# A block of x loaded by itself, a stored block without its identity matmul, and the first chunk's scores packed into 15 batches for 16

## The chip, the cores and the metric

One core of a Trainium2 chip runs the kernel. The metric is the device time of one execution in microseconds (us). The kernel before took 268.93 us (median of 3 runs, 268.72 to 268.98). A program on one core has no second die to compare with. All medians below are of runs that were classed fast.

## The reference, cut to what matters

```python
def reference(A_x, A_wqkv, A_wo, B_x, B_w_gate, B_w_up, B_w_down):
    xn = _layernorm(A_x)                         # x: 1 x 2048 x 512, bf16
    # attention: 32 heads of 16, each query sees itself and the 255 keys before it
    q, k, v = split(xn @ wqkv)
    p = softmax(where(0 <= i - j < 256, q k^T / 4, -1e9))
    # gated block without a nonlinearity, F = 1792
    return A_x + (p v) @ wo + ((xn @ w_gate) * (xn @ w_up)) @ w_down
```

## The kernel before

The sequence is worked on in four chunks of 512 rows. In each chunk there are four groups `c` of eight heads. The scores of one group are computed in *batches*: up to 512 columns of queries against 64-key pieces, written to one PSUM tile `S` of four banks. ScalarE takes the exp of the whole tile into a strip `P`. GpSimd then cuts the far edge of the window (two instructions for each far block) and VectorE the diagonal.

```python
FIRST = (((5, 5, 7), (0, 0, 4)), ((3, 3, 5), (1, 1, 5)),
         ((3, 6, 7), (7, 7, 7), (2, 2, 6)), ((4, 4, 7), (6, 6, 7)))   # (key piece, first and last query block)

def scores(self, T, c, pieces):
    S = self.s_tiles.tile([128, 4, 512], F32, tag="S", name="S")     # one buffer
    ...                                                              # 16 small-tile matmuls for each piece
    P = self.ppool.tile([128, 4, 512], BF16, tag="P", name="P")      # seven buffers
    nc.scalar.activation(out=P[:, :, 0:col], in_=S[:, :, 0:col], func=ACT.Exp, scale=0.25)
    for at in self.places(pieces, 4):
        for half in (slice(0, 64), slice(64, 128)):
            self.triangle(P[half, :, at:at + 64], False)             # GpSimd: the far masks
```

All other matmuls (projections, gate, up, down, output) are *fillers*: a list that a small scheduler puts between the score batches when the program is built. It does so by estimated cost, so that the fillers are spread evenly over the batches:

```python
total = sum(w[0] for w in work) - RESERVE + SCORES * len(steps) + VALUES * (len(due) - 1)
for g, s in enumerate(steps):
    self.scores(*s)
    upto = total * (g + 1) / len(steps)
    ...
    fill(upto, g)               # fillers until the estimate says `upto`
    self.mask_diag(*s)
```

One filler of cost 0 opens the next chunk. It takes the chunk's tiles and has GpSimd fill the ones columns and the padding of `V`. The value projections come just behind it, and ScalarE copies their results into the other columns of `V`:

```python
def new_chunk(self, T):
    ...
    nc.gpsimd.memset(self.heads(self.V[T])[:, :, :, 16:18], 1.0)     # "the fills"
    nc.gpsimd.memset(self.V[T][:, VW - 16:], 0.0)
    nc.gpsimd.memset(self.VS[T][:, SW - 16:], 0.0)

def proj_v(self, t, ks=range(4)):
    ps = self.bank(ks, "vp")                                         # one of four PSUM banks ("M")
    ...                                                              # four matmuls
    nc.scalar.activation(out=heads(V[T])[...][:, :, :, 0:16], in_=ps, func=ACT.Copy)

def project(T):                                                      # in the list of fillers
    add(0, lambda: self.new_chunk(T))
    for b in range(4):
        ... proj_v ...
    ... proj_qk ...

gu(T, ...)                                                           # the gate and up matmuls of chunk T
if T + 1 < NCH:
    project(T + 1)
```

The softmax here doesn't subtract the row's maximum and nothing guards it: scores larger than these inputs give would overflow.

Of the kernel before, what the change touches and what calls it, by code (L numbers as in the profile page):

```python
# [7 lines left out]
BF16 = mybir.dt.bfloat16  # L8
# [7 lines left out]
BIG = 2.0 ** 126  # L16
VW = 4 * 32 * 18 + 16
SW = 4 * 16 * 18 + 16
FIRST = (((5, 5, 7), (0, 0, 4)), ((3, 3, 5), (1, 1, 5)),
         ((3, 6, 7), (7, 7, 7), (2, 2, 6)), ((4, 4, 7), (6, 6, 7)))  # L20
LATER = (((-2, 0, 2), (0, 0, 4)), ((5, 5, 7), (1, 1, 5)), ((-3, 0, 1), (7, 7, 7), (3, 3, 7)),
         ((-4, 0, 0), (6, 6, 7), (2, 2, 6)), ((-1, 0, 3), (4, 4, 7)))
ACT_FREE = 11


class Kernel:
# [26 lines left out]
    def setup(self):  # L53
        nc, const, NT, NF = self.nc, self.const, self.NT, self.NF
        self.x = const.tile([128, NT, 512], BF16, name="x")
        self.Wqkv = const.tile([128, 4, 1536], BF16, name="Wqkv")
        self.Wo = const.tile([128, 4, 512], BF16, name="Wo")
        self.Wg = const.tile([128, 4, self.F], BF16, name="Wg")
        self.Wu = const.tile([128, 4, self.F], BF16, name="Wu")
        self.Wd = const.tile([128, NF, 512], BF16, name="Wd")  # L60
        xv = self.x_d.rearrange("(t p) d -> p t d", p=128)
        wq = self.w_d["qkv"].rearrange("(k p) n -> p k n", p=128)
        wg = self.w_d["g"].rearrange("(k p) n -> p k n", p=128)
        wu = self.w_d["u"].rearrange("(k p) n -> p k n", p=128)
        for lo, hi in ((0, 1), (1, 4)):
            nc.sync.dma_start(out=self.x[:, lo:hi, :], in_=xv[:, lo:hi, :])
        for lo in (1024, 512, 0):
            nc.sync.dma_start(out=self.Wqkv[:, :, lo:lo + 512], in_=wq[:, :, lo:lo + 512])
        h = self.F // 2
        for lo in (0, h):  # L70
            nc.sync.dma_start(out=self.Wg[:, :, lo:lo + h], in_=wg[:, :, lo:lo + h])
            nc.sync.dma_start(out=self.Wu[:, :, lo:lo + h], in_=wu[:, :, lo:lo + h])
            if lo == 0:
                nc.sync.dma_start(out=self.x[:, 4:8, :], in_=xv[:, 4:8, :])
        nc.sync.dma_start(out=self.Wd[:], in_=self.w_d["d"].rearrange("(f p) n -> p f n", p=128))
        nc.sync.dma_start(out=self.Wo[:], in_=self.w_d["o"].rearrange("(c p) n -> p c n", p=128))
        nc.sync.dma_start(out=self.x[:, 8:NT, :], in_=xv[:, 8:NT, :])

        warm = const.tile([128, 1], F32, name="warm")
        nc.vector.memset(warm[:], 0.0)  # L80
        nc.scalar.activation(out=warm[:], in_=warm[:], func=ACT.Exp)
        ident = const.tile([128, 128], BF16, name="ident")
        nc.gpsimd.memset(ident[:], 0.0)
        nc.gpsimd.affine_select(out=ident[:], in_=ident[:], compare_op=ALU.not_equal, fill=1.0,
                                base=0, pattern=[[-1, 128]], channel_multiplier=1)
        self.ident = ident
        wps = self.ps_m.tile([128, 128], F32, tag="M", name="wps")
        for _ in range(38):
            nc.tensor.matmul(wps[:], lhsT=ident[:], rhs=ident[:], start=True, stop=True)
        pi = const.tile([128, 1], I32, name="pi")  # L90
        nc.gpsimd.iota(pi[:], pattern=[[0, 1]], base=0, channel_multiplier=1)
        podd = const.tile([128, 1], I32, name="podd")
        nc.vector.tensor_scalar(out=podd[:], in0=pi[:], scalar1=4, scalar2=1,
                                op0=ALU.arith_shift_right, op1=ALU.bitwise_and)
        self.odd = const.tile([128, 1], F32, name="odd")
        nc.vector.tensor_copy(out=self.odd[:], in_=podd[:])
        self.mhalf = const.tile([128, 4], F32, name="mhalf")
        nc.gpsimd.memset(self.mhalf[:], -0.5)
        self.diag = const.tile([128, 64], BF16, name="diag")
        self.far = const.tile([128, 64], BF16, name="far")  # L100
        nc.gpsimd.memset(self.diag[:], BIG)
        nc.gpsimd.memset(self.far[:], BIG)
        for half in (slice(0, 64), slice(64, 128)):
            self.triangle(self.diag[half], True)
            self.triangle(self.far[half], False)
        self.xnT, self.Q, self.hT, self.O, self.OT = {}, {}, {}, {}, {}
        self.K, self.Ko, self.V, self.VS = {}, {}, {}, {}
        self.strips, self.at = {}, {}

    def new_chunk(self, T):  # L110

# [135 lines left out]
        self.proj_qk(0, 1, 1)  # L247


    def scores(self, T, c, pieces):  # L250

        nc = self.nc
        S = self.s_tiles.tile([128, 4, 512], F32, tag="S", name="S")
        col = 0
        for m, q0, q1 in pieces:
            U, j = divmod(8 * T + m, 8)
            keys, q, n = slice(64 * j, 64 * j + 64), 64 * q0, 64 * (q1 - q0 + 1)
            for par in range(2):
                for e in range(4):
                    rows = slice(32 * e, 32 * e + 16 + 16 * par)  # L260
                    nc.tensor.matmul(S[64 * par:64 * par + 64, e, col:col + n],  # L261
                                     lhsT=(self.Ko if par else self.K)[U][rows, c, keys],
                                     rhs=self.Q[T][rows, c, q:q + n],
                                     start=True, stop=True, tile_position=(32 * e, 64 * par),
                                     skip_group_check=True)
            col += n
        P = self.ppool.tile([128, 4, 512], BF16, tag="P", name="P")
        nc.scalar.activation(out=P[:, :, 0:col], in_=S[:, :, 0:col], func=ACT.Exp, scale=0.25)  # L268
        self.strips[(T, c, pieces)] = P
        for at in self.places(pieces, 4):  # L270
            for half in (slice(0, 64), slice(64, 128)):
                self.triangle(P[half, :, at:at + 64], False)

    def places(self, pieces, far):

        out, at = [], 0
        for m, q0, q1 in pieces:
            out += [at + 64 * (q - q0) for q in range(q0, q1 + 1) if q == m + far]
            at += 64 * (q1 - q0 + 1)
        return out  # L280

    def mask_diag(self, T, c, pieces):

        P = self.strips[(T, c, pieces)]
        places = [at // 64 for at in self.places(pieces, 0)]
        step = places[1] - places[0] if len(places) == 2 else 1
        v = P.rearrange("p e (b x) -> p e b x", x=64)[:, :, places[0]:places[-1] + 1:step, :]
        n = len(places)
        self.nc.vector.tensor_tensor(out=v, in0=v, op=ALU.min,  # L289
                                     in1=self.diag.unsqueeze(1).unsqueeze(1).to_broadcast([128, 4, n, 64]))  # L290

    def values(self, T, c, accs=None):
# [2 lines left out]
        nc = self.nc  # L295
        if accs is None:
            accs = [self.ps_m.tile([128, 512], F32, tag="M", name="acc") for _ in range(2)]
        todo = []
        for pieces in LATER if T else FIRST:
            P, col = self.strips.pop((T, c, pieces)), 0  # L300
            for m, q0, q1 in pieces:
                todo.append((P, col, m, 64 * q0, 64 * (q1 - q0 + 1)))
                col += 64 * (q1 - q0 + 1)
        for i, (P, col, m, q, n) in enumerate(todo):
            U, j = divmod(8 * T + m, 8)
            b, h = divmod(j, 2)
# [99 lines left out]
    def fillers(self):  # L406


        out = []
        NCH, NF = self.NCH, self.NF  # L410

        def add(cost, f, before=None, after=None):
            out.append((cost, f, before, after))
# [65 lines left out]
        T = NCH - 1  # L479
        for b in range(4):  # L480
            down(T, b)
            if b < 3:
                wo(T, b, (0, 1, 2))
            if b in (1, 3):
                add(1, lambda b=b: self.add_x(T, b, 0 if b == 1 else 1))
        return [(*o, None, None)[:4] for o in out]

    def run(self):
# [5 lines left out]
        self.first_chunk()  # L494
        steps, self.first, self.last = [], {}, {}
        for T in range(NCH):
            for c in range(4):
                self.first[T, c] = len(steps)
                for pieces in LATER if T else FIRST:
                    self.last[T, c] = len(steps)  # L500
                    steps.append((T, c, pieces))
        due = {g: key for key, g in self.last.items()}
        SCORES, VALUES = 1.85, 5.5
        self.beside = {}
# [2 lines left out]
        spent, n, scored = 0, 0, 0  # L507
# [44 lines left out]
        T = NCH - 1  # L552
# [10 lines left out]
        fill(spent + 15, -1)  # L563
        for b in range(3):
            self.wo(T, b, (3,))
            self.store(T, b, on_act=(b == 1))
        fill(10 ** 9, -1)
        assert n == len(work)
        self.wo(T, 3, (0, 1, 2, 3))
# [39 lines left out]
```

## Time and profile before

| what | value | read from |
|---|---|---|
| device time, median | 268.93 us | timed runs |
| span of the profiled run (its device time 269.22) | 267.5 us | page |
| TensorE busy | 258.4 us, 97% | page, part 1 |
| 512-column matmuls, start to start | 0.2155 us | TensorE timeline |
| a score batch of 512 columns between fillers | 0.10 + 0.35 us | TensorE timeline |
| idle time of ScalarE before value copies, until GpSimd's fills | 1.4 us in all | waits |

Three lines of the page of the kernel before: the span, the first part (busy us, share of the span, instructions of each engine; PEld is the weight load) and the chain of waits by engine.

```profile
span 267.5 us, 8861 instructions
...
PE 258.4 (97%) x3860; PEld 119.1 (45%) x3882; DVE 181.7 (68%) x352; ACT 170.6 (64%) x132; POOL 113.8 (43%) x281
...
PE 88%; DVE 7%; issue 1%; DMA 1%; ACT 1%; SPq 0%; POOL 0%; DVEq 0%; POOLq 0%
```

TensorE is busy nearly all the time and is most of the chain, so the time is what TensorE needs before it is saturated, plus its work, plus the tail, plus any gaps.

The head, from the timeline of the kernel before. Columns: start, duration, engine, line, operation, output and inputs, count, and in brackets the idle time before it and what ended it. An entry that stands for several instructions runs from the first start to the last end, with others in between.

```profile
2.86 0.69 DVE L148 BATCH_NORM_STATS2 st<-x 128x6 f32<-128x512 bf16 x1 [1.02 <-DMA x<-in_A_x_dram]
...
4.80 0.70 DVE L148 BATCH_NORM_STATS2 st<-x 128x6 f32<-128x512 bf16 x1 [0.84 <-DMA x<-in_A_x_dram]
...
5.63 0.38 DVE L168 TENSOR_SCALAR xn<-x,mv,rs 128x512 bf16<-128x512 bf16 x1
...
7.25 0.40 PE L186 MATMUL xTp<-ident,xn 128*128 128x128 bf16 x4 [0.79 <-DVE xn L168]
...
7.49 0.81 PE L200 MATMUL vp<-Wqkv,xnT 128*128 128x512 bf16 x3
```

The statistics of block 1 (the second `st`) start at 4.80 us, after 0.84 us of waiting for the transfer of blocks 1 to 3. Block 0 is normalized only behind them (5.63), and TensorE is saturated from the second block's transposes (7.25) on.

### The profile page before, as it was taken

How to read it: one execution, taken by the hardware profiler on the slowest of the kernel's cores; microseconds unless marked ns; L12 is line 12 of the kernel's file. 1: busy time of each engine (PE TensorE's matmuls, PEld its weight loads, DVE VectorE, ACT ScalarE, POOL GpSimd, SP SyncE). 2: the span in 40 equal slices, each digit the busy share in tenths (PEclk: the TensorE clock that was granted, in tenths of full speed). 3: DMA queues.
4: the chain of work that ended last, by engine and by line, in shares of the span. 5: the costliest groups of instructions: out<-in, count | busy, mean ns of one | idle time of the engine just before them, and what ended most of it. 6: DMA issues, size and time to landing. Idle time of an engine off the chain costs nothing.

```text
span 267.5 us, 8861 instructions
## 1 busy us (share of the span) xinstructions
PE 258.4 (97%) x3860; PEld 119.1 (45%) x3882; DVE 181.7 (68%) x352; ACT 170.6 (64%) x132; POOL 113.8 (43%) x281
## 2 busy tenths in 40 slices
PE   6899999999999999999999999999999999999994
PEld 6444434444444444444444444444444444434453
DVE  4377898958756859676674868857762575978251
ACT  2675658696556776769656676668765667665500
POOL 5215333422674533345556433545444353443500
PEclk9999999999999999999999999999999999999999
DMA  6999911120023000001014100000200010000002
GB/s 205 373 358 334 250 22 22 23 47 0 4 61 81 20 2 4 2 2 44 5 23 97 43 0 5 0 4 2 44 5 20 26 39 2 2 0 2 4 2 81
DMA packets 19336, 15.13 MB, mean 57 GB/s; under 512 B 7264, under 2 KB 19296, under 8 KB 19296
## 3 DMA queue, kind: packets, MB, share of 16 engines
q1 hardware_dynamic: 18464, 14.09, 18.1%
q8 instruction: 30, 0.49, 0.7%
q10 hardware_dynamic: 832, 0.46, 0.6%
q14 instruction: 10, 0.08, 0.1%
HBM read 9.70 MB, written 2.10 MB: 44 GB/s over the span
## 4 chain that ended last, share of the span: by engine, by line
PE 88%; DVE 7%; issue 1%; DMA 1%; ACT 1%; SPq 0%; POOL 0%; DVEq 0%; POOLq 0%
PE up L359 17%; PE gp L345 17%; PE psd L378 16%; PE qkp L212 11%; PE S L261 9%; PE acc L316 6%; PE psd L384 5%; PE vp L200 4%; PE L L378 2%; DMA x<-in_A_x_dram 1%; DVE hT L363 1%; DVE st L148 1%; DVE at L322 1%; DVE gsb L353 1%; DVE xn L168 1%
## 5 line engine op out<-in xcount | busy, mean ns | idle before, releaser
L268 ACT ACTIVATE P<-S 128x2048 bf16<-128x2048 f32 x76 | 141.0, 1855 | 57.4 <-PE S L261 49.9
L137 POOL TENSOR_SCALAR_AFFINE_SELECT P<-P 64x256 bf16<-64x256 bf16 x224 | 97.3, 434 | 128.9 <-ACT P L268 118.2
L345 PE MATMUL gp<-xnT,Wg 128*128 128x512 bf16 x224 | 60.0, 380 | 0.1
L359 PE MATMUL up<-xnT,Wu 128*128 128x512 bf16 x224 | 59.6, 380 | 0.0
L378 PE MATMUL psd<-Wd,hT 128*128 128x512 bf16 (+1 forms) x198 | 48.7, 368 | 1.4 <-issue 1.3
L363 DVE TENSOR_TENSOR hT<-up,gsb 128x512 bf16<-128x512 f32 x56 | 38.4, 686 | 16.0 <-PE up L359 14.4
L289 DVE TENSOR_TENSOR P<-P,diag 128x512 bf16<-128x512 bf16 (+1 forms) x76 | 30.6, 404 | 10.4 <-ACT P L268 10.4
L322 DVE STREAM_TRANSPOSE at<-acc 128x512 f32<-128x512 f32 x30 | 19.7, 695 | 19.7 <-PE acc L316 19.7
L378 PEld LDWEIGHTS <-hT 128*128 128x128 bf16 x238 | 21.6, 98 | 25.3 <-issue 2.6
L359 PEld LDWEIGHTS <-Wu 128*128 128x128 bf16 x224 | 20.4, 98 | 25.3 <-issue 2.5
L345 PEld LDWEIGHTS <-Wg 128*128 128x128 bf16 x224 | 20.3, 98 | 25.5 <-issue 2.7
L261 PE MATMUL S<-Q,K 16*64 16x320 bf16 (+1 forms) x720 | 31.2, 260 | 0.4
L261 PE MATMUL S<-Q,Ko 32*64 32x320 bf16 (+1 forms) x720 | 31.1, 260 | 0.0
L212 PE MATMUL qkp<-xnT,Wqkv 128*128 128x512 bf16 x128 | 30.0, 380 | 0.0
L261 PEld LDWEIGHTS <-K 16*64 16x64 bf16 x720 | 12.2, 103 | 32.2 <-issue 32.2
L353 DVE CAST gsb<-gp 128x512 bf16<-128x512 f32 x36 | 24.5, 681 | 2.6 <-PE gp L345 1.3
L351 ACT ACTIVATE gsb<-gp 128x512 bf16<-128x512 f32 x20 | 11.9, 597 | 11.8 <-PE gp L345 11.1
L316 PE MATMUL acc<-P,VS 64*32 64x320 bf16 (+4 forms) x672 | 18.9, 254 | 0.0
L316 PE MATMUL acc<-P,V 64*32 64x320 bf16 (+4 forms) x672 | 18.4, 254 | 0.1
L212 PEld LDWEIGHTS <-Wqkv 128*128 128x128 bf16 x128 | 11.7, 98 | 14.5 <-issue 1.4
L384 PE MATMUL psd<-Wo,OT 128*128 128x512 bf16 (+1 forms) x55 | 15.5, 368 | 0.6 <-issue 0.6
L316 PEld LDWEIGHTS <-V 64*32 64x32 bf16 x720 | 14.5, 90 | 2.8 <-issue 2.4
(55 smaller groups left out, 194.1 us busy)
## 6 DMA issues: line engine op xcount, KB each, us to landing
Wg<-in_B_w_gate_dram SPq DMA_DIRECT2D x2, 896.0 KB, 10.4
Wu<-in_B_w_up_dram SPq DMA_DIRECT2D x2, 896.0 KB, 13.0
Wd<-in_B_w_down_dram SPq DMA_DIRECT2D x1, 1792.0 KB, 17.3
out_dram<-y SPq DMA_DIRECT2D x14, 128.0 KB, 1.8
Wqkv<-in_A_wqkv_dram SPq DMA_DIRECT2D x3, 512.0 KB, 6.4
x<-in_A_x_dram SPq DMA_DIRECT2D x1, 1024.0 KB, 10.9
VS<-V SPq DMA_DIRECT2D x6, 144.0 KB, 2.6
x<-in_A_x_dram SPq DMA_DIRECT2D x1, 512.0 KB, 11.4
```

Of the source, the lines that this page charges most:

```text
L137: nc.gpsimd.affine_select(out=v, in_=v, pattern=pattern + [[1 if diag else -1, 64]], compare_op=ALU.is_ge if diag else ALU.is_gt, fill=0.0 ...
L212: nc.tensor.matmul(ps[:], lhsT=self.Wqkv[:, k, lo:lo + 128], rhs=self.xnT[T][:, :, k, :], start=(k == 0), stop=(k == 3))
L261: nc.tensor.matmul(S[64 * par:64 * par + 64, e, col:col + n], lhsT=(self.Ko if par else self.K)[U][rows, c, keys], rhs=self.Q[T][rows, c, ...
L268: nc.scalar.activation(out=P[:, :, 0:col], in_=S[:, :, 0:col], func=ACT.Exp, scale=0.25)
L289: self.nc.vector.tensor_tensor(out=v, in0=v, op=ALU.min, in1=self.diag.unsqueeze(1).unsqueeze(1).to_broadcast([128, 4, n, 64]))
L316: nc.tensor.matmul(accs[par][32 * e:32 * e + 32, q:q + n], lhsT=v, rhs=P[rows, e, col:col + n], start=(i == 0), stop=(i == len(todo) - 1), ...
L345: nc.tensor.matmul(ps[:], lhsT=self.Wg[:, k, 128 * f:128 * f + 128], rhs=self.xnT[T][:, :, k, :], start=(k == 0), stop=(k == 3))
L353: nc.vector.tensor_copy(out=self.gsb[:], in_=ps[:])
L359: nc.tensor.matmul(ps[:], lhsT=self.Wu[:, k, 128 * f:128 * f + 128], rhs=self.xnT[T][:, :, k, :], start=(k == 0), stop=(k == 3))
L363: nc.vector.tensor_tensor(out=self.hT[T][:, f, :], in0=ps[:], in1=self.gsb[:], op=ALU.mult)
L378: nc.tensor.matmul(ps, lhsT=self.hT[T][:, f, 128 * b:128 * b + 128], rhs=self.Wd[:, f, c0:c1], start=(f == 0), stop=False)
L384: self.nc.tensor.matmul(ps, lhsT=self.OT[T][:, c, 128 * b:128 * b + 128], rhs=self.Wo[:, c, c0:c1], start=False, stop=(c == 3))
```

## The change

The intent is three savings: x block 1 arrives sooner because it is loaded by itself; one output block gets x added by VectorE when it is stored, instead of by an identity matmul on TensorE; and the first chunk's short batches (384 columns) are packed together over head groups, so that 15 full batches do the work of 16.

```diff
-FIRST = (((5, 5, 7), (0, 0, 4)), ((3, 3, 5), (1, 1, 5)),
-         ((3, 6, 7), (7, 7, 7), (2, 2, 6)), ((4, 4, 7), (6, 6, 7)))
+SHARED = ((5, 5, 7), (0, 0, 4)), ((3, 3, 5), (1, 1, 5)), ((3, 6, 7), (7, 7, 7), (2, 2, 6))
+FOUR, SIX = (4, 4, 7), (6, 6, 7)
+REST = (((0, *SIX), (1, *SIX), (0, *FOUR)), ((1, *FOUR), (2, *FOUR)), ((2, *SIX), (3, *SIX), (3, *FOUR)))
 ...
-        for lo, hi in ((0, 1), (1, 4)):
+        for lo, hi in ((0, 1), (1, 2), (2, 4)):
             nc.sync.dma_start(out=self.x[:, lo:hi, :], in_=xv[:, lo:hi, :])
 ...
+    def batches(self, T):
+        out = []
+        for c in range(4):
+            out += [tuple((c, *p) for p in pieces) for pieces in (LATER if T else SHARED)]
+            if T == 0 and c < 3:
+                out.append(REST[c])
+        return out
 ...                                  # scores, places, mask_diag, values: a piece carries its group
-            if b in (1, 3):
-                add(1, lambda b=b: self.add_x(T, b, 0 if b == 1 else 1))
+        add(1, lambda: self.add_x(T, 3, 1))
 ...
-            self.store(T, b, on_act=(b == 1))
+            self.store(T, b)
```

More of the change, by code (lines that the diff above doesn't have):

```diff
@@ L107, in setup @@
         self.K, self.Ko, self.V, self.VS = {}, {}, {}, {}
-        self.strips, self.at = {}, {}
+        self.strips, self.parts, self.at = {}, {}, {}
     def new_chunk(self, T):
@@ L247, in first_chunk, with scores @@
         self.proj_qk(0, 1, 1)
-    def scores(self, T, c, pieces):
+    def batches(self, T):
[5 more added lines that the diff above has]
+        return out
+    def scores(self, T, pieces):
         nc = self.nc
         S = self.s_tiles.tile([128, 4, 512], F32, tag="S", name="S")
+        P = self.ppool.tile([128, 4, 512], BF16, tag="P", name="P")
         col = 0
-        for m, q0, q1 in pieces:
+        for c, m, q0, q1 in pieces:
             U, j = divmod(8 * T + m, 8)
@@ L265, in scores @@
                                      skip_group_check=True)
+            self.parts.setdefault((T, c), []).append((P, col, m, q, n))
             col += n
-        P = self.ppool.tile([128, 4, 512], BF16, tag="P", name="P")
         nc.scalar.activation(out=P[:, :, 0:col], in_=S[:, :, 0:col], func=ACT.Exp, scale=0.25)
-        self.strips[(T, c, pieces)] = P
+        self.strips[(T, pieces)] = P
         for at in self.places(pieces, 4):
@@ L276, in places @@
         out, at = [], 0
-        for m, q0, q1 in pieces:
+        for _, m, q0, q1 in pieces:
             out += [at + 64 * (q - q0) for q in range(q0, q1 + 1) if q == m + far]
@@ L280, in places, with mask_diag @@
         return out
-    def mask_diag(self, T, c, pieces):
-        P = self.strips[(T, c, pieces)]
+    def mask_diag(self, T, pieces):
+        P = self.strips.pop((T, pieces))
         places = [at // 64 for at in self.places(pieces, 0)]
-        step = places[1] - places[0] if len(places) == 2 else 1
+        n = len(places)
+        step = places[1] - places[0] if n > 1 else 1
+        assert places == list(range(places[0], places[-1] + 1, step))
         v = P.rearrange("p e (b x) -> p e b x", x=64)[:, :, places[0]:places[-1] + 1:step, :]
-        n = len(places)
         self.nc.vector.tensor_tensor(out=v, in0=v, op=ALU.min,
@@ L297, in values @@
             accs = [self.ps_m.tile([128, 512], F32, tag="M", name="acc") for _ in range(2)]
-        todo = []
-        for pieces in LATER if T else FIRST:
-            P, col = self.strips.pop((T, c, pieces)), 0
-            for m, q0, q1 in pieces:
-                todo.append((P, col, m, 64 * q0, 64 * (q1 - q0 + 1)))
-                col += 64 * (q1 - q0 + 1)
+        todo = self.parts.pop((T, c))
         for i, (P, col, m, q, n) in enumerate(todo):
@@ L496, in run @@
         for T in range(NCH):
-            for c in range(4):
-                self.first[T, c] = len(steps)
-                for pieces in LATER if T else FIRST:
+            for pieces in self.batches(T):
+                for c, *_ in pieces:
+                    self.first.setdefault((T, c), len(steps))
                     self.last[T, c] = len(steps)
-                    steps.append((T, c, pieces))
+                steps.append((T, pieces))
         due = {g: key for key, g in self.last.items()}
```

## The prediction

> **What bounds the kernel.** TensorE. The page gives it 258.4 of 267.5 us (97%), at full clock; VectorE has 68%, ScalarE 64%. The chain of waits is 88% TensorE. In its timeline, 512-column matmuls start 0.2155 us apart; from the second block's transposes (7.25 us) to the last output matmuls (263.8 us) I find almost no gap except the switches into and out of the small-tile score and value batches (other stalls: about 0.4 us). So time = head (7.25 us until TensorE is saturated) + TensorE's work + tail (3.7 us).
>
> **What the change does.**
>
> 1. *Head.* The first transpose waits for normalized block 0 (6.06 us), which VectorE makes only after the statistics of block 1; these waited for the 384 KB transfer of blocks 1 to 3 (VectorE idle 0.84 us, to 4.80 us; timeline). A 128 KB transfer lands in 2.0 us (DMA issues) and an issue costs 0.4 us, so block 1 alone should land at about 3.3 us. Its statistics then start when VectorE is free (3.95 us), 0.85 us earlier, and the second transposes at about 6.4 us. Blocks 2 and 3, needed at about 5.1 us, should land at about 4.8. The value weights landed 4.5 us after their issue at 1.72, at about 6.2 us; one more issue ahead makes that up to 6.6, and the first value matmul wants them at about 6.65: close. Estimate: 0.7 us (0.3 to 0.85), kept whole, as TensorE is saturated after it.
>
> 2. *Packing.* The first chunk's 16 score batches (12 of 512 columns, 4 of 384) become 15 of 512, with the same pieces. A 512-column batch holds TensorE for 0.45 us between its neighbours (timeline), a 384-column one for 0.40: 4 x 0.40 + 12 x 0.45 - 15 x 0.45 = 0.25 us saved. What is saved is a switch: the Trainium skill, "TensorEngine Tiling (Array Packing)", Key Properties, says a change of tiling mode drains the engine; the gap of 0.1 us before each batch agrees. ScalarE saves 4 x 1.451 + 12 x 1.878 - 15 x 1.878 = 0.17 us, VectorE one mask: off the path.
>
> 3. *Identity matmul.* One 512-column matmul goes: 0.22 us. Its block's store moves from ScalarE (0.60 us) to VectorE (0.69 us). VectorE does stores 0 and 2 from 260.0 to 261.3 us, then idles 2.47 us until the last block: a third fits.
>
> 4. *Moved.* Fillers slide by up to a batch, and evacuations change engines: ScalarE takes 23 gate copies for 20. Some 0.2 us of stalls may come or go. One strip lives longer, just inside the 7 buffers.
>
> Sum: 0.7 + 0.25 + 0.22 = 1.2 us. **Predicted: 267.7 us**, 8 in 10 within 267.0 to 268.6. Chances: faster by over 2% 0.01; within 2% 0.98; slower 0.01.
>
> **What would show it.** Head: statistics of block 1 at about 3.95 us, first value matmul at about 6.7 for 7.49. Packing: 75 exps, all 128x2048, and no new TensorE gap from 20 to 50 us. Identity: one identity matmul left in the tail, and the time from the last value matmuls to the end unchanged. Span about 266.3 us.
>
> **What would make it wrong.** Value weights or blocks 2 and 3 land later because of the added transfer, and the head's gain shrinks to 0.3 us or nothing. A packed batch waits for another head group's Q or K, or values of group 0 for the bigger third mask. The shifted evacuations stall TensorE for more than 0.3 us, or the third VectorE store, its transfer now on the one queue, delays the last output.

## More of the kernel before

The opening of chunk 2 in the kernel before, cut from the timeline: TensorE's value projections `vp`, GpSimd's masks and fills, ScalarE's copies to `V`, the exp behind the first copy, and the next scores.

```profile
116.10 1.47 PE L200 MATMUL vp<-Wqkv,xnT 128*128 128x512 bf16 x5
...
116.97 0.89 POOL L137 TENSOR_SCALAR_AFFINE_SELECT P<-P 64x256 bf16<-64x256 bf16 x2 [1.18 <-ACT P L268]
...
117.86 2.33 PE L200 MATMUL vp<-Wqkv,xnT 128*128 128x512 bf16 x10
...
117.92 0.33 POOL L118 MEMSET V<- 128x256 bf16 x1
...
118.28 0.60 ACT L204 ACTIVATE V<-vp 128x512 bf16<-128x512 f32 x1 [1.38 <-POOL V L118]
...
118.78 1.87 ACT L268 ACTIVATE P<-S 128x2048 bf16<-128x2048 f32 x1
...
120.70 0.22 PE L261 MATMUL S<-Q,K 16*64 16x64 bf16 x4
```

ScalarE waits for the first fill (`MEMSET V`), which is done just after the two masks of the last batch. The copy starts at 118.28, 1.4 us after ScalarE was free. One line of the waits (engine and line, waiting for what: us in total, times, longest) shows that it is the only wait of a value copy for the fills that this profile has (1.4 us, once):

```profile
ACT V L204 <- POOL V L118: 1.4, 1, 1.4
```

## The result, and the profile after

| | median | runs | ratio to before (95%) |
|---|---|---|---|
| before | 268.96 us | 4, 268.72 to 268.98 | |
| changed | 270.73 us | 4, 270.61 to 270.81 | 1.0068 (1.005 to 1.0085) |

The changed kernel is correct and 1.8 us slower, where 1.2 us faster was forecast.

The same lines of the page of the changed kernel:

```profile
span 268.9 us, 8864 instructions
...
PE 258.2 (96%) x3861; PEld 119.0 (44%) x3881; DVE 179.9 (67%) x348; ACT 171.9 (64%) x134; POOL 113.9 (42%) x281
...
PE 80%; issue 7%; POOL 5%; ACT 4%; DVE 2%; DMA 1%; POOLq 0%; ACTq 0%
```

TensorE has the same work (258.2 us busy) in a longer span, and its share of the chain fell from 88% to 80%: there are gaps now. The head is not where they are. The timeline of the changed kernel's head, to be read against the one of before:

```profile
3.90 0.68 DVE L149 BATCH_NORM_STATS2 st<-x 128x6 f32<-128x512 bf16 x1
...
6.35 0.40 PE L187 MATMUL xTp<-ident,xn 128*128 128x128 bf16 x4 [0.55 <-DVE xn L169]
...
6.62 0.81 PE L201 MATMUL vp<-Wqkv,xnT 128*128 128x512 bf16 x3
```

The statistics of block 1 start at 3.90 for 4.80 us, and TensorE is saturated 0.9 us earlier (6.35 for 7.25), as forecast.

To find the gaps I went through TensorE's order block by block. Between two score or value batches, the fillers should take 0.2155 us for each 512-column matmul plus 0.10 us for the switch to small tiles. Some matmul records are missing from a trace, so I took the number of matmuls from the program's order and only the start times of the batches from the trace. Stretches of fillers past the head that took over 0.25 us more than that:

| kernel | stretches (start: us lost) |
|---|---|
| before | none (largest 0.23 at 36.6; 0.15 at 117.9) |
| changed | 118.1: 1.69; 183.3: 1.78 |

So the whole loss is in two places, 3.47 us in sum, and both are where value projections of chunks 2 and 3 begin. Here is the first of them in the timeline of the changed kernel, the counterpart of the stretch shown of before:

```profile
115.04 2.75 PE L201 MATMUL vp<-Wqkv,xnT 128*128 128x512 bf16 x11
...
116.75 1.91 POOL L138 TENSOR_SCALAR_AFFINE_SELECT P<-P 64x256 bf16<-64x256 bf16 x4 [2.15 <-ACT P L279]
...
118.09 1.04 PE L201 MATMUL vp<-Wqkv,xnT 128*128 128x512 bf16 x4
118.71 0.33 POOL L119 MEMSET V<- 128x256 bf16 x1
...
119.07 1.57 ACT L205 ACTIVATE V<-vp 128x512 bf16<-128x512 f32 x3 [2.39 <-POOL V L119]
119.72 1.89 PE L213 MATMUL qkp<-xnT,Wqkv 128*128 128x512 bf16 x8 [0.60 <-ACT V L205]
...
120.52 1.90 ACT L279 ACTIVATE P<-S 128x2048 bf16<-128x2048 f32 x1
...
122.47 0.30 PE L272 MATMUL S<-Q,K 16*64 16x256 bf16 x4 [0.86 <-ACT P L279]
```

Read it upwards from the end. The scores at 122.47 wait 0.86 us for the exp that has to empty their one PSUM tile. That exp (120.52) stands on ScalarE behind value copies, which start at 119.07 after 2.39 us of waiting for GpSimd. (By the code, fills and copies write different columns of `V`, 16 and 17 of each head and 0 to 15; in the trace the copy waits for the fill all the same.) GpSimd's fill takes 0.33 us but starts only at 118.71, because four masks of the batch before (1.91 us, from 116.75, when their exp was done) stand ahead of it. Meanwhile the value projections have filled the four PSUM banks, and the next projection (`qkp`) waits 0.60 us for a bank. At 183 us the same happens once more. The view of the tile `V` of the changed kernel from 100 to 200 us sums both (line, engine, operation, count: duration in ns, first and last start; then who waited for this tile, us and times):

```profile
L119 POOL MEMSET V<- x2: 327/328/328, 118.7 to 184.5; 128x256 bf16 x2
...
who waited for it (us, times):
  ACT V L205: 4.8, 2
  PE qkp L213: 0.9, 2
```

ScalarE waited 4.8 us for the fills, in two waits, against one of 1.4 us before. The profile puts only 0.9 us of TensorE's waiting down to the copies (`PE qkp`); most of the rest, 2.1 us in the waits of the whole run, is booked under the exp that came late behind them.

Nothing in the diff touches the fills. Their place in GpSimd's order is what moved. The order of GpSimd's instructions, as the program is built (one mask is one GpSimd instruction on a strip; statistics left out, the masks in between summed up from the end of the first chunk's norms):

```
before:   ... 38 masks, fills of chunk 2, 14 masks ... 38 masks, fills of chunk 3, 74 masks
changed:  ... 42 masks, fills of chunk 2, 10 masks ... 42 masks, fills of chunk 3, 70 masks
```

The scheduler's `upto` depends on the number of batches and on the sum of the filler costs, and the change alters both. So every filler slid against the batches, and the two openings came to stand behind a batch with four masks. The value projections slid too: those of chunk 2 start 1.06 us earlier (115.04 for 116.10), so the copies are due earlier while the first fill comes 0.8 us later (118.71 for 117.92). e1 and e5 below move the fills alone. This list could be had before the prediction was made; I read it then and did not follow it up.

### The profile page after: what moved, and what is told of

It is laid out like the page before. It is cut to its first block, busy times and chain, and to the rows that moved or that the text cites. A ratio compares the mean times of both kernels' runs of the same rounds, so it can differ in the third digit from the quotient of the medians.

```text
span 268.9 us, 8864 instructions
## 1 busy us (share of the span) xinstructions
PE 258.2 (96%) x3861; PEld 119.0 (44%) x3881; DVE 179.9 (67%) x348; ACT 171.9 (64%) x134; POOL 113.9 (42%) x281
## 4 chain that ended last, share of the span: by engine, by line
PE 80%; issue 7%; POOL 5%; ACT 4%; DVE 2%; DMA 1%; POOLq 0%; ACTq 0%
PE psd L385 16%; PE gp L352 15%; PE up L366 14%; PE qkp L213 10%; PE S L272 9%; PE acc L323 6%; POOL P L138 5%; PE psd L391 5%; ACT P L279 3%; PE vp L201 2%; PE L L385 2%; ACT V L205 1%; DVE st L149 1%; DMA x<-in_A_x_dram 1%; PE L L391 1%
## 5 line engine op out<-in xcount | busy, mean ns | idle before, releaser
L301 DVE TENSOR_TENSOR P<-P,diag 128x512 bf16<-128x512 bf16 (+1 forms) x75 | 30.0, 401 | 9.2 <-ACT P L279 9.2
L272 PE MATMUL S<-Q,K 16*64 16x320 bf16 (+4 forms) x720 | 31.0, 260 | 2.1 <-ACT P L279 2.1
L272 PE MATMUL S<-Q,Ko 32*64 32x320 bf16 (+4 forms) x720 | 31.0, 260 | 0.0
L272 PEld LDWEIGHTS <-K 16*64 16x64 bf16 x720 | 12.3, 103 | 33.8 <-issue 33.8
L360 DVE CAST gsb<-gp 128x512 bf16<-128x512 f32 x33 | 22.6, 683 | 3.0 <-PE gp L352 2.0
L358 ACT ACTIVATE gsb<-gp 128x512 bf16<-128x512 f32 x23 | 13.7, 597 | 13.1 <-PE gp L352 11.9
L391 PE MATMUL psd<-Wo,OT 128*128 128x512 bf16 (+1 forms) x59 | 16.2, 369 | 0.2 <-issue 0.2
```

Source lines behind the costliest of these rows:

```text
L272: nc.tensor.matmul(S[64 * par:64 * par + 64, e, col:col + n], lhsT=(self.Ko if par else self.K)[U][rows, c, keys], rhs=self.Q[T][rows, c, ...
L301: self.nc.vector.tensor_tensor(out=v, in0=v, op=ALU.min, in1=self.diag.unsqueeze(1).unsqueeze(1).to_broadcast([128, 4, n, 64]))
L360: nc.vector.tensor_copy(out=self.gsb[:], in_=ps[:])
L391: self.nc.tensor.matmul(ps, lhsT=self.OT[T][:, c, 128 * b:128 * b + 128], rhs=self.Wo[:, c, c0:c1], start=False, stop=(c == 3))
```

## The experiments

The theory (F): the loss is the fills' place behind four masks in GpSimd's order; none of the three parts costs anything by itself. Rivals: (P) the fillers slid so that value copies stand behind an exp on ScalarE, whatever the fills do; (Q) the packed batches cost something and only they do.

### e1: the changed kernel with the fills issued early

```diff
 def project(T):
-    add(0, lambda: self.new_chunk(T))
     for b in range(4):
 ...
+            if T + 1 < NCH:
+                add(0, lambda T=T: self.new_chunk(T + 1))
             gu(T, norms(1, 1, 3) if T == 0 else {})
```

The order of instructions on TensorE, ScalarE, VectorE and the DMA queue is identical to that of the changed kernel; only GpSimd's differs.

> The changed kernel, with GpSimd's three fills of the next chunk's V and VS (ones and zero pad) issued ahead of the gate work of the chunk before, instead of just before that chunk's value projections. The order of instructions on TensorE, ScalarE, VectorE and the DMA queue is the same as in the changed kernel. Theory F (the fills sit behind four masks of a score batch in GpSimd's order, so the V evacuations on ScalarE, the four PSUM banks and TensorE wait for them twice, 1.69 and 1.78 us lost at 118 and 183 us): both losses go, 267.3 us (267.0 to 267.7), ratio to before 0.994. Rival P (the packed batches moved the filler work against the score batches, and the value evacuations stand behind an exp on ScalarE; the fills do not matter): same as the changed kernel, 270.7 us.

Measured: 267.83 us median of six runs (267.51 to 270.9), ratio to before 0.9985 (0.995 to 1.002). Five of the six lie between 267.51 and 268.12; the sixth, 270.9, makes the interval wide. The median is 0.1 us above the range expected; P's 270.7 is refuted. (The changed kernel was timed in other rounds, beside a kernel before of nearly the same time, 268.96 there and 268.81 here.) The timeline of e1 at the same stretch:

```profile
115.04 2.75 PE L201 MATMUL vp<-Wqkv,xnT 128*128 128x512 bf16 x11
...
116.57 1.08 ACT L205 ACTIVATE V<-vp 128x512 bf16<-128x512 f32 x2
...
118.96 1.89 PE L213 MATMUL qkp<-xnT,Wqkv 128*128 128x512 bf16 x8
```

The value copies start at 116.57 for 119.07 us, with the same orders on the other engines, and `qkp` follows at 118.96 for 119.72 with no wait. The view of the tile `V` of e1 has one set of fills between 100 and 200 us, at 151.0 us, early, and nobody under "who waited":

```profile
L119 POOL MEMSET V<- x1: 330/330/330, 151.0 to 151.0; 128x256 bf16 x1
...
who waited for it (us, times):
busy tenths in 40 slices 0000000000000000920909009093900000000000
```

By the same count as above, no stretch past the head lost more than 0.13 us. The span fell by 3.5 us (268.9 to 265.4), which is the 3.47 us of the two stretches.

### e2: the packing alone, on the kernel before

Edit: the first part of the diff only (with the x load and the identity matmul as before).

> The kernel before with the packing alone. Its GpSimd order has both sets of fills behind four more masks, as in the changed kernel. Theory F: -0.25 us for the batch saved and +3.4 us for the two stalls, 272.1 us (271.5 to 272.5). Rival Q (the packing costs nothing and the stalls come from the interplay with the other two parts): 268.7 us.

Measured: 271.81 us (4 runs, 271.57 to 271.96), ratio 1.0109 (1.0096 to 1.0122). The packing alone makes the kernel 3.0 us slower, as F had it, and its GpSimd order is that of the changed kernel. Its stretches: 118.7, 2.31 us lost; 184.6, 1.29 us lost. Q's 268.7 is refuted for the packing alone, but a packing that itself costs something is not yet out.

### e3: the identity matmul alone, on the kernel before

```diff
-            if b in (1, 3):
-                add(1, lambda b=b: self.add_x(T, b, 0 if b == 1 else 1))
+        add(1, lambda: self.add_x(T, 3, 1))
 ...
-            self.store(T, b, on_act=(b == 1))
+            self.store(T, b)
```

This takes one matmul away, near the end (253.9 us in the kernel before), and it changes the sum of filler costs by one unit. That is enough to put the last set of fills, and only that, behind 42 masks for 38.

> The kernel before with the identity matmul alone taken out (its store on VectorE). Its GpSimd order has only the last set of fills behind four more masks. Theory F: -0.22 us for the matmul and +1.75 us for one stall, at about 184 us and none at 118: 270.5 us (270.0 to 270.8). Rival Q (only the packing brings stalls): 268.7 us.

Measured: 270.59 us median (6 runs, 270.39 to 272.11), ratio 1.0073 (1.0056 to 1.009): slower by 1.8 us for one matmul less, with no packed batch in it. Q is refuted. The timeline of e3 at the opening of chunk 3:

```profile
182.96 2.10 POOL L137 TENSOR_SCALAR_AFFINE_SELECT P<-P 64x256 bf16<-64x256 bf16 x4 [2.58 <-ACT P L268]
...
183.87 1.04 PE L200 MATMUL vp<-Wqkv,xnT 128*128 128x512 bf16 x4
...
185.12 0.33 POOL L118 MEMSET V<- 128x256 bf16 x1
...
185.48 1.57 ACT L204 ACTIVATE V<-vp 128x512 bf16<-128x512 f32 x3 [2.58 <-POOL V L118]
186.12 1.89 PE L212 MATMUL qkp<-xnT,Wqkv 128*128 128x512 bf16 x8 [1.21 <-ACT V L204]
...
188.87 0.30 PE L261 MATMUL S<-Q,K 16*64 16x256 bf16 x4 [0.86 <-ACT P L268]
```

It is the same picture as in the changed kernel: four masks, the fill, the copies, then TensorE. The stretch from 183.87 lost 2.31 us; at 118 no stretch lost as much as 0.15 us.

### e4: x block 1 by itself, alone, on the kernel before

```diff
-        for lo, hi in ((0, 1), (1, 4)):
+        for lo, hi in ((0, 1), (1, 2), (2, 4)):
```

> The kernel before with x block 1 loaded by itself and nothing else; the order on TensorE, ScalarE, VectorE and GpSimd is that of before. All theories: no new stall, the head's 0.87 us kept whole: 268.1 us (267.9 to 268.3), ratio 0.9968.

Measured: 268.4 us median (5 runs, 268.33 to 268.8), ratio 0.9986 (0.9974 to 0.9998). There is no new stall, but the gain is 0.4 us, half of what the two profiles show. This expectation missed; e8 takes it up.

### e5: the fills made slower, on the kernel before

```diff
-        nc.gpsimd.memset(self.heads(self.V[T])[:, :, :, 16:18], 1.0)
+        for _ in range(7 if T else 1):
+            nc.gpsimd.memset(self.heads(self.V[T])[:, :, :, 16:18], 1.0)
```

> The kernel before with the first of the three GpSimd fills (the ones columns of V) repeated 7 times for chunks 1 to 3, about 1.6 us more of GpSimd work at that place; the order on TensorE, ScalarE and VectorE is that of before. Theory F: the fills of chunk 2 end at about 119.9 for 118.3 us, the exp behind the first V evacuation and the next scores go with them, about 1.6 us of TensorE lost at 118; at 52 us (0.5 us late) and 183 us (an exp runs until 183.1 anyway) nothing or little: 270.4 us (269.7 to 271.2). Rival P (fills do not matter): 268.8 us.

Measured: 273.24 us median (4 runs: two at 272.3, two at 274.2), ratio 1.0147 (1.0108 to 1.0186). The kernel before can be made slow by later fills alone, with the orders on TensorE, ScalarE and VectorE untouched, which is what F says; P is refuted a second time. The size missed: the seven fills take 2.64 us from the first start to the last end. I had reckoned about 1.9, with one every 0.26 us; they follow each other every (2.64 - 0.33) / 6 = 0.385 us. The timeline of e5:

```profile
118.28 2.33 PE L201 MATMUL vp<-Wqkv,xnT 128*128 128x512 bf16 x10
...
118.33 2.64 POOL L119 MEMSET V<- 128x256 bf16 x7
...
121.01 0.60 ACT L205 ACTIVATE V<-vp 128x512 bf16<-128x512 f32 x1 [3.69 <-POOL V L119]
...
121.66 0.59 PE L213 MATMUL qkp<-xnT,Wqkv 128*128 128x512 bf16 x2 [1.04 <-ACT V L205]
...
123.42 0.22 PE L262 MATMUL S<-Q,K 16*64 16x64 bf16 x4 [1.18 <-ACT P L269]
```

The copy waits until 121.01, the projection until 121.66 and the scores until 123.42: 2.45 us lost in this stretch, and 0.28 and 0.37 us in those at 52 and 187 us. The count leaves out what is lost inside value batches; from score batch to score batch, the opening of chunk 1 lost about 0.8 us in all, where nothing or little was expected. Why two of the four runs are 1.8 us above the others was not found; the profiled run is one of the faster two.

### e6: the fills issued early, on the kernel before

The edit of e1 on the kernel before.

> The kernel before with the fills issued ahead of the gate work of the chunk before, as in e1. Theory F: the kernel before lost only 0.15 us at 118 to this wait, so 268.65 us (268.4 to 268.8); the gain of e1 is the repair of what the change broke, not a gain that the place of the fills brings by itself. Rival: if the early place helps in some other way, it gains here what it gained on the changed kernel, 3 us: 265.8 us.

Measured: 268.47 us median (6 runs, 268.34 to 268.48) beside 268.99 for before on that chip, ratio 0.9969 (0.9943 to 0.9995). The kernel before ran less steadily there (268.67 to 270.6), so the median difference of 0.5 us says little more than "a few tenths". The same edit that gained about 3 us on the changed kernel gains a few tenths here: it repairs what the change broke.

### e7: e1 once more

> The same as e1, for a second interval, since one of its six runs was 3.3 us above the others: 267.6 us (267.4 to 267.9), ratio 0.9955, and no run near 270.9 if that was chance.

Measured: 267.61 us median (6 runs, 267.49 to 268.24), ratio 0.994 (0.9916 to 0.9965). This is the fastest kernel, faster than before and than the changed one by 1.4 and 3.1 us. (The changed kernel was timed in other rounds, so the 3.1 is a difference of medians.) No run came near 270.9 here, and the kernel before had two such excursions (270.54 and 270.6) in the same rounds, so a single high run is nothing peculiar to e1.

The profiled run was the slowest of the six (268.24), and its head shows why. First the timeline of e7's head, then the spread of the landing times of the three Wqkv transfers, from their issue:

```profile
2.19 1.57 SPq L70 DMA_DIRECT2D Wqkv<-in_A_wqkv_dram  x3
...
3.86 0.68 DVE L150 BATCH_NORM_STATS2 st<-x 128x6 f32<-128x512 bf16 x1
...
6.30 0.40 PE L188 MATMUL xTp<-ident,xn 128*128 128x128 bf16 x4 [0.79 <-DVE xn L170]
...
7.42 1.02 PE L202 MATMUL vp<-Wqkv,xnT 128*128 128x512 bf16 x4 [0.73 <-ACT xnT L189]
```

```profile
DMA to landing us min/median/max: 5.1/6.1/7.0
```

The statistics of block 1 and the transposes are as early as ever (3.86 and 6.30 us), but the first value matmul starts at 7.42 us (6.62 in the changed kernel). The profile names ScalarE's `xnT`, whose two copies had ended by about 6.1 us (they are 0.66 us long from 5.44, and not shown); the other operand is the value part of Wqkv. It is the first of the three transfers issued from 2.19 us on. The shortest landing of 5.1 us is its own (the same view, cut down to the issue of that one transfer, gives 5.1), so it came at 7.3 us; in the profile of e1 it took 4.3 us and came at 6.5. This is the collision that the prediction called close; it cost 0.8 us here and nothing in the profile of e1.

### e8: a second profile of the kernel before

> The kernel before unchanged, for a second profile. Splitting the x load gained 0.9 us in the profile and 0.4 us in the timed runs (e4). If the profile of before fell on a late landing of x blocks 1 to 3, the statistics of block 1 start here at about 4.4 us for 4.80, with a span of about 267.1. If the landing is always at 4.80, the missing 0.5 us is elsewhere.

Measured: 268.82 us (one run, so its state is unknown), span 267.1. The eleven timed runs of the kernel before on that chip had spans of 267.0 to 267.6, but for the two high ones. The timeline of its head:

```profile
2.93 0.69 DVE L149 BATCH_NORM_STATS2 st<-x 128x6 f32<-128x512 bf16 x1 [1.09 <-DMA x<-in_A_x_dram]
...
4.39 0.69 DVE L149 BATCH_NORM_STATS2 st<-x 128x6 f32<-128x512 bf16 x1 [0.36 <-DMA x<-in_A_x_dram]
...
7.07 1.03 PE L201 MATMUL vp<-Wqkv,xnT 128*128 128x512 bf16 x4
```

Blocks 1 to 3 landed at about 4.39 us for 4.80, and the first value matmul started at 7.07 for 7.49. The profile on which the prediction was made fell on a late landing. Against this one, the split is worth 0.4 to 0.5 us, which is what e4 measured.

## Why the prediction was wrong

**The step that failed** is number 4: "Fillers slide by up to a batch, and evacuations change engines: ScalarE takes 23 gate copies for 20. Some 0.2 us of stalls may come or go." What moved and mattered was not the gate copies but the three fills on GpSimd. They came to stand behind four masks twice, ScalarE waited 4.8 us for them where it had waited 1.4, and TensorE lost 3.47 us in two stretches, where it had lost 0.15 us at the one and nothing at the other. That e1 restores the time by moving the fills alone, with every other engine's order untouched, shows it; that e3 brings one stall without any packing, and e5 brings a stall without any of the three parts, shows that it is not the packing. The prediction's own list of what would make it wrong had "The shifted evacuations stall TensorE for more than 0.3 us": that is what happened, to the copies of the value projections, but it was left at 0.2 us and the fills that hold these copies back were not named.

**Head.** The mechanism was right (3.90 us for 3.95 forecast, first value matmul 6.62 for 6.7). The size was off: 0.7 us was forecast, 0.4 measured (e4), because the profile of before had a late landing that its timed runs did not share (span 267.5 there, 267.1 in e8). The late value weights of e7's profiled run took 0.8 us; that is one run, and no part of the 0.4.

**Packing.** The 75 exps are all 128x2048 and no gap arose from 20 to 50 us, as forecast. The size was forecast too small. The traces give it: from the start of the first score batch to that of the second batch of chunk 1, with the fillers in between taken off at 0.2155 us for each 512-column matmul, the profiles without packing (before, e3, e4, e6, e8) have 10.62 to 10.63 us and those with it (changed, e1, e2, e7) 9.99 to 10.00 (e5 is left out, as its slow fills fall into this part). So the packing saves 0.63 us: the 0.25 forecast, and about 0.4 more, because the kernel before lost 0.23 us at 36.6 and 0.30 us in the value batch at 43 us, and the changed kernel in this part no more than 0.13. Why these small waits go was not looked into.

As a check, the span of e1 is 1.2 us shorter than that of e4 (265.4 and 266.6): 0.63 for the packing, 0.22 for the identity matmul, 0.13 for the fills (the stretch at 117 us in e4) and 0.2 from the last value batch to the end make 1.2. The repaired kernel (e7) is 1.4 us faster than the kernel before, near the 1.2 forecast for the changed one; but that is partly luck, as a head forecast 0.3 too high and a packing forecast 0.4 too low nearly cancel.

**Identity matmul.** The third store on VectorE was free, as forecast: from the first matmul of the last value batch to the end it took 12.5 us before (255.02 to 267.5) and 12.3 in the changed kernel (256.59 to 268.9). (e2 and e6, whose store was left on ScalarE, also have 12.3, so the 0.2 us is not the store's gain.)

**What the skill said.** The Trainium skill, "TensorEngine Tiling (Array Packing)", Key Properties, has a tiling switch drain the engine; the 0.10 us before every score batch of this trace agrees. And "TensorE: Matmul & The Clock Gate", Step-by-step: what each phase is for, says that TensorE is the only engine that reorders. That sentence holds the whole case: on GpSimd a short fill cannot pass the masks ahead of it, and those wait for an exp. The trace agrees: the fill, 0.33 us long, started at 118.71, right behind the four masks from 116.75. It had no need to come so late: in e1 it stands tens of microseconds earlier.

**Left open.** In e1 and e7 the device time is 2.1 us longer than the span, in the other kernels 1.7; so in device time the repair brings about 3 us of the 3.5 that the spans show. What the 0.4 us outside the span is was not found. Nor was the cause of e5's runs at 274 us and of the single high runs of several kernels (270.5 to 272.1).

## What to carry to other kernels

When a change moves work in a program whose order comes out of a scheduler, compare the order of *every* engine, also of one that is only 43% busy, and ask of each short instruction that others wait for: what stands ahead of it now? Issue such preparation (fills, constants, pads) long before its use, on any in-order engine whose other work waits for results; in e6 it cost nothing, and it takes the luck out of the schedule. (It needs a free buffer that early: the pool of `V` has three.) And a wait for a transfer read from one profile is one draw: take a second profile before counting its full length as a gain.

## What the Trainium skill lacked or had wrong

- "GPSIMD Engine Reference" and "Perfetto Trace Analysis": I found no warning in them that a cheap GpSimd instruction can gate TensorE by its place in its engine's order. Here fills of 0.33 us cost 3.5 us of span (e1 against the changed kernel).
- "TensorEngine Tiling (Array Packing)", Key Properties: it says that a switch drains the engine, but gives no size. Here a 512-column score batch between full-array matmuls held TensorE for 0.45 us, while one full-array matmul of 512 columns takes 0.2155 us; a 384-column batch held it for 0.40.
- "DMA: Bandwidth & Descriptors", Anatomy of one DMA: it gives a fixed 2.0 us plus bytes over 436 GB/s, measured for the GpSimd path, which as an estimate makes 2.9 us for 384 KB; it has no such fit for SyncE's queue. From there, with other transfers under way, 384 KB took 3.5 us in one profile of the kernel before and 3.1 in the next; the 0.4 us between them is about what the gain of e4 fell short of the 0.87 us expected.
